# A six-layer cross network on one core: two row blocks stored singly, seventeen row loads, and narrower remainder evictions

## The chip, the core and the metric

The kernel runs on one core of a Trainium2 chip. A core has several engines that run their own instruction streams side by side: TensorE (PE) multiplies matrices into PSUM, VectorE (DVE) does elementwise work, ScalarE (ACT) does elementwise work and here mostly copies PSUM into SBUF ("evicts" it), GpSimd (POOL) does a little setup, and SyncE (SP) issues DMA transfers. Sixteen DMA engines carry the transfers. The metric is the device time of one execution in microseconds (us), taken as the median of several runs.

## The reference

The input x0 has 4096 rows and 416 columns (26 fields of 16). There are six weight matrices of 416 x 416 and six bias rows. All is bf16.

```python
def reference(x0, ws, bs):
    x = x0
    for l in range(ws.shape[0]):
        x = x0 * (x @ ws[l] + bs[l]) + x
    return x
```

Each layer multiplies the state x with a weight matrix, adds a bias, multiplies elementwise with x0 and adds the state of before.

## The kernel before, in words

The kernel doesn't carry x from layer to layer but a factor c with x = x0 * c: c starts from 1 and each layer adds the product and the bias to it. So a layer is three steps: TensorE forms x @ ws[l] in PSUM; ScalarE evicts it with the bias added (tile `t`); VectorE adds it to c and multiplies c by x0 to get the next x.

In layers 0 to 4 the data is transposed: columns of x lie on the 128 partitions, batch rows along the free dimension. The 416 columns are three full groups of 128 (index `m`, tiles `XM0`, `XH`, `CM`) and a remainder of 32 (tiles `XR`, `CR`). The 4096 batch rows are two halves (index `s`), each of four runs of 512 (index `g`). The remainder of 32 columns is packed: the four runs of one half lie on four blocks of 32 partitions, so that the remainder of a half is one tile of 128 x 512.

Layer 0 is `first_layer`, layers 1 to 3 are the loop with `layer_products`, `ew_main` (the full groups) and `ew_rem` (the remainder), and layer 4 is `feeding_layer`, which also sends the finished c through DMA transposes into row order (`XLrows`).

In layers 1 to 3 the order is: two products (one for each of the first two tiles) with their evictions, then `rem_pair`, which forms the remainder products of both halves in one PSUM tile of two banks and then runs `ew_rem` for each half, and then the other four tiles. `ew_rem` (lines 190 to 204) evicts the 512 columns of a half in pieces of `n` columns (line 197), and then VectorE adds all 512 columns to `CR` (line 203) and multiplies them (line 204). Before the change the pieces are 256 columns, and 128 for half 1 in layers 1 and 2. PSUM is used as four tiles of two banks, in turn, so the tile of the remainder products is taken again by the second tile of products after it; TensorE's first write into it there is a row product (line 215).

Layer 5 (`l = LL`) is formed in row order, 128 batch rows to a PSUM bank: 32 row blocks in four rounds of eight banks. For each row block the steps are a product on TensorE (lines 464 to 481), a copy out of PSUM by ScalarE (line 519, in the first round line 496), an addition of the row-ordered c (`XLrows`, line 523), a multiplication with the x0 rows (`X0rows`, line 505), and a store (line 508). The x0 rows come through a loop of loads at line 133, issued on SP behind the loads of the weights.

Several things set the order of the work. VectorE's instructions in the last layer and a few others are pinned to program order (`pin`). The rest is ordered by the framework's scheduler, by dependence and planned time, when the program is built. The multiplication and store of a row block are put off by one step: `close_product` runs when the next row block has been evicted and added. Stores are issued on SP, the very last one on ScalarE's queue. Transfers take eight completion semaphores in turn, and a transfer first waits for the one that had its semaphore before.

In the last round (`final`, `q` of 6) the row blocks are closed one by one. A tile `o` holds two of them, and before the change blocks 0 and 1, 2 and 3, 4 and 5 share a tile and a store; blocks 6 and 7 have their own. The lines that decide this are:

```python
paired = final and u < 6
j = u % 2 if paired else 0
if not j:
    outs.append(opool.tile([P, 2, D], BF16, name="o"))
```

`j` is the place in the tile, and the store is issued with the second of a pair or with a single block. Blocks 5, 6 and 7 get their c added on TensorE (lines 468 and 470), so VectorE only multiplies there, and block 7 is multiplied straight out of PSUM.

Of the kernel before, what the change touches and what calls it, by code (L numbers as in the profile page):

```python
# [16 lines left out]
def kernel(  # L17
# [16 lines left out]
    CW = 512  # L34
    SW = NG * CW
    NBT = B // P
# [36 lines left out]
    def load_wm(eng, l):  # L73
        eng.dma_start(WM[:, l], ws[l, 0:NK * P, :].rearrange("(k p) n -> p k n", p=P))
# [5 lines left out]
    def pin(ins):  # L80
        tc.keep_in_program_order(ins)
# [46 lines left out]
        load_wr(nc.sync, g, 1, L)  # L128
    for l in range(2, L):
        load_wm(nc.sync, l)  # L130
    for q in range(18):
        b0, b1 = NBT * q // 18, NBT * (q + 1) // 18
        nc.sync.dma_start(X0rows[:, b0:b1, :], x0_v[:, b0:b1, :])
    for g in range(NG):
        nc.sync.dma_start(bLr[32 * g:32 * g + 1, :], bs[LL:LL + 1, :])
# [55 lines left out]
    def ew_rem(l, s, pr, nxtR):  # L191
        cols = slice(CW * s, CW * s + CW)
        halves = [slice(a, a + CW // 2) for a in range(0, CW, CW // 2)]
        base = CR[:, cols] if l == 0 else tpool.tile([P, 2 * CW], BF16, name="t")
        n = CW // (4 if s and l in (1, 2) else 2)
        for a in range(0, CW, n):
            nc.scalar.activation(base[:, a:a + n], pr[:, a:a + n], ACT.Identity, bias=bR[:, l:l + 1], scale=1.0)  # L197
        if l == 0:
            for a in halves:
                part = slice(CW * s + a.start, CW * s + a.stop)  # L200
                pin(nc.vector.tensor_tensor(out=nxtR[:, part], in0=CR[:, part], in1=XR[0][:, part], op=ALU.mult))
            return
        nc.vector.tensor_tensor(out=CR[:, cols], in0=base[:, 0:CW], in1=CR[:, cols], op=ALU.add)
        nc.vector.tensor_tensor(out=nxtR[:, cols], in0=CR[:, cols], in1=XR[0][:, cols], op=ALU.mult)
# [30 lines left out]
    def first_layer(s):  # L235
# [53 lines left out]
        for m in range(2):  # L289
            ew_main(0, s, m, 1, pb[m], nxt)  # L290
        ew_rem(0, 0, pr[:, 0, :], nxtR)
        ew_main(0, s, 2, 1, pb[2], nxt)
        ew_rem(0, 1, pr[:, 1, :], nxtR)

    bias_setup()
# [4 lines left out]
    def rem_pair(l, cur, curR, nxtR):  # L300
        pr2 = psum.tile([P, 2, CW], FP32, tag="ps", name="pr2")
        for s in range(NS):
            mm_rem(l, s, pr2[:, s, :], cur, curR)
        for s in range(NS):
            ew_rem(l, s, pr2[:, s, :], nxtR)
# [140 lines left out]
    l = LL  # L446
# [8 lines left out]
    def mm_q_open(q, g, py):  # L455
        for k in range(NK):
            for j in range(0, P, 32):
                nc.tensor.matmul(py[j:j + 32, 0:D], lhsT=q_x(q, g, k)[:, j:j + 32], rhs=WM[:, l, k, :],  # L458
                                 start=(k == 0), stop=False, tile_position=(0, j))

    def mm_q_full(q, g, py, closes, adds=False):
        s, i = quads[q]
        for k in range(NK):
            nc.tensor.matmul(py[:, 0:D], lhsT=q_x(q, g, k), rhs=WM[:, l, k, :],  # L464
                             start=((not closes) and k == 0), stop=(closes and not adds and k == NK - 1))
            if adds:
                c0 = col0(s, g) + 128 * i
                nc.tensor.matmul(py[:, P * k:P * k + P], lhsT=CM[:, k, c0:c0 + 128], rhs=ident[:], start=False, stop=False)
        if adds:
            nc.tensor.matmul(py[:, NK * P:D], lhsT=CR[:, CW * s + 128 * i:CW * s + 128 * i + 128],  # L470
                             rhs=ident[:, 32 * g:32 * g + 32], start=False, stop=True)

    def mm_q_rem(q, py, done):
        s, i = quads[q]
        biased = q == NQ - 1
        for g in range(NG):
            nc.tensor.matmul(py[g][:, 0:D], lhsT=curR[32 * g:32 * g + 32, CW * s + 128 * i:CW * s + 128 * i + 128],  # L477
                             rhs=WR[32 * g:32 * g + 32, l, :], start=(g >= done), stop=(not biased and g < done),
                             tile_position=(32 * g, 0))
        for g in range(NG if biased else 0):  # L480
            nc.tensor.matmul(py[g][:, 0:D], lhsT=ones[32 * g:32 * g + 1, :],
                             rhs=bLr[32 * g:32 * g + 1, :], start=False, stop=(g < done), tile_position=(32 * g, 0))
# [10 lines left out]
    def evict_quad(u, src):  # L493
        q, g0 = u // 4, u % 4
        w = wide[:, q, 0:NG * D].rearrange("p (g d) -> p g d", g=NG)
        nc.scalar.copy(w[:, g0:g0 + 2, :], src)
        if g0 + 2 == NG:
            close_product()
            pin(nc.vector.tensor_tensor(out=w, in0=w, in1=XLrows[:, rows(q, 0, NG), :], op=ALU.add))
            pending.append((w, q, 0, NG, w, 0, True, nc.sync))  # L500
# [9 lines left out]
    def ew(q, g0, srcs, o, j, last, eng, added, direct):  # L510
        if direct:
            close_product()
            pending.append((srcs[0], q, g0, 1, o, j, last, eng))
            return
        t = tpool.tile([P, 2 * CW], BF16, name="t")
        n = 0
        for src in srcs:
            w = src.shape[1]
            nc.scalar.copy(t[:, n * D:n * D + w * D].rearrange("p (a d) -> p a d", a=w), src)  # L519
            n += w  # L520
        tv = t[:, 0:n * D].rearrange("p (a d) -> p a d", a=n)
        if not added:
            pin(nc.vector.tensor_tensor(out=tv, in0=tv, in1=XLrows[:, rows(q, g0, n), :], op=ALU.add))  # L523
        close_product()
        pending.append((tv, q, g0, n, o, j, last, eng))
# [5 lines left out]
    for q, at, done in rounds:  # L531
        tiles = [psum.tile([P, 2, CW], FP32, tag="ps", name=f"py{n}") for n in range(4)]
        bank = [tiles[n][:, a, :] for n, a in at]

        final = q + 2 == NQ

        def close(groups):
            u = groups[0][0]
            srcs = [tiles[at[g[0]][0]][:, at[g[0]][1]:at[g[0]][1] + len(g), 0:D] for g in groups]
            if q == 0:  # L540
                evict_quad(u, srcs[0])
                return
            paired = final and u < 6
            j = u % 2 if paired else 0
            if not j:
                outs.append(opool.tile([P, 2, D], BF16, name="o"))
            ew(q + u // 4, u % 4, srcs, outs[-1], j, bool(j) or not paired, nc.scalar if final and u == 7 else nc.sync,
               final and u >= 5, final and u == 7)

        for u in range(done):  # L550
            if q == 0:
                mm_q_open(q, u, bank[u])
            else:
                mm_q_full(q, u, bank[u], False)
        mm_q_rem(q, bank[0:4], done)
        close([range(done)])
        mm_q_rem(q + 1, bank[4:8], 0)
        for u in range(done, 8):
            mm_q_full(q + u // 4, u % 4, bank[u], True, final and u >= 5)
            if at is ENDS:  # L560
                close([[u]])
            elif u % 2:
                close([[u - 1, u]] if at is PAIRS else [[u - 1], [u]])
                if q == 0 and u == 3:
                    last_rows_out()
# [31 lines left out]
```

## Time and profile before

| what | value |
|---|---|
| median of the runs shown | 128.73 us (128.63 to 128.79, 3 runs) |
| the profiled execution | 129.13 us |
| its span in the trace | 127.3 us |
| TensorE busy | 122.9 us, 97% of the span |
| VectorE busy | 102.3 us, 80% |
| ScalarE busy | 88.2 us, 69% |
| DMA | 16.37 MB, 129 GB/s over the span |
| mean granted TensorE clock | 0.995 of full speed |

The span runs from the first to the last instruction in the trace; the execution's own time is longer by what lies around it. "Busy" is time in which an engine runs an instruction; being busy doesn't mean that the engine decides the time. The chain is followed backward from the last instruction, at each step to what released it. Lines such as L197 are line numbers of the kernel. A line of the time order reads: start, duration, engine, line, operation, output and input tiles, how many were merged, and in brackets the idle time ahead of it with what ended it. "SPq" and "ACTq" are those engines' instructions that issue transfers.

### The profile page before, as it was taken

How to read it: one execution, taken by the hardware profiler on the slowest of the kernel's cores; microseconds unless marked ns; L12 is line 12 of the kernel's file. 1: busy time of each engine (PE TensorE's matmuls, PEld its weight loads, DVE VectorE, ACT ScalarE, POOL GpSimd, SP SyncE). 2: the span in 40 equal slices, each digit the busy share in tenths (PEclk: the TensorE clock that was granted, in tenths of full speed). 3: DMA queues.
4: the chain of work that ended last, by engine and by line, in shares of the span. 5: the costliest groups of instructions: out<-in, count | busy, mean ns of one | idle time of the engine just before them, and what ended most of it. 6: DMA issues, size and time to landing. Idle time of an engine off the chain costs nothing.

```text
span 127.3 us, 3935 instructions
## 1 busy us (share of the span) xinstructions
PE 122.9 (97%) x1682; PEld 55.2 (43%) x1682; DVE 102.3 (80%) x188; ACT 88.2 (69%) x113; POOL 5.2 (4%) x18
## 2 busy tenths in 40 slices
PE   7999999999999999999999999999999999999980
PEld 3243343354435444534453444344435445445450
DVE  0023679774989898998898998898999999999990
ACT  0047866896869486869485859495859698679760
POOL 4004000500000000000000000000000000000000
PEclk9999999999999999999999999999999999999998
DMA  3999999999880000000000000000049999999865
GB/s 82 238 233 225 186 236 250 306 332 323 253 262 17 5 0 0 8 0 5 0 5 0 5 0 0 5 0 5 0 80 140 197 104 231 171 248 322 268 224 178
DMA packets 42229, 16.37 MB, mean 129 GB/s; under 512 B 31034, under 2 KB 42212, under 8 KB 42212
## 3 DMA queue, kind: packets, MB, share of 16 engines
q1 hardware_dynamic: 37432, 15.40, 53.2%
q10 hardware_dynamic: 4780, 0.72, 3.7%
q8 instruction: 13, 0.21, 0.8%
q14 instruction: 4, 0.03, 0.1%
HBM read 6.15 MB, written 3.41 MB: 75 GB/s over the span
## 4 chain that ended last, share of the span: by engine, by line
PE 88%; DVE 5%; DMA 2%; ACT 1%; DVEq 1%; issue 1%
PE pt L209 50%; PE ph L241 13%; PE py L464 6%; PE pt L215 5%; PE pr L225 5%; PE wps L148 4%; DVE o L505 2%; DVE t L523 2%; DMA out_dram<-XH 2%; PE pr L221 2%; PE ph L248 2%; PE py L458 1%; PE py L477 1%; ACT t L519 1%; DVEq L592 1%
## 5 line engine op out<-in xcount | busy, mean ns | idle before, releaser
L209 PE MATMUL pt<-XH,WM 128*32 128x512 bf16 x1152 | 65.2, 379 | 0.0
L187 ACT ACTIVATE t<-pt,bM 128x1024 bf16<-128x1024 f32 x36 | 37.1, 1114 | 13.1 <-PE pt L215 13.1
L209 PEld LDWEIGHTS <-WM 128*32 128x32 bf16 x1152 | 29.7, 97 | 33.8 <-issue 5.1
L188 DVE TENSOR_TENSOR CM<-t,CM 128x1024 bf16<-128x1024 bf16 x36 | 24.7, 687 | 4.3 <-ACT t L187 4.3
L189 DVE TENSOR_TENSOR XH<-CM,XM 128x1024 bf16<-128x1024 bf16 x36 | 24.9, 692 | 2.6
L464 PE MATMUL py<-WM,XH 128*128 128x416 bf16 x90 | 17.0, 339 | 0.0
L241 PE MATMUL ph<-XM,WM 128*128 128x512 bf16 x72 | 16.5, 381 | 0.0
L333 ACT ACTIVATE t<-pt,bM 128x1024 bf16<-128x1024 f32 x12 | 12.4, 1114 | 4.1 <-PE pt L215 4.1
L181 ACT ACTIVATE CM<-ph,bM 128x1024 bf16<-128x1024 f32 x12 | 12.5, 1112 | 3.5 <-PE ph L248 3.5
L519 ACT CAST t<-py 128x416 bf16<-128x416 f32 (+1 forms) x18 | 10.8, 601 | 3.3 <-PE py L464 1.4
L183 DVE TENSOR_TENSOR XH<-CM,XM 128x512 bf16<-128x512 bf16 x24 | 8.8, 429 | 4.1 <-ACT CM L181 4.1
L464 PEld LDWEIGHTS <-XH 128*128 128x128 bf16 x90 | 8.5, 98 | 7.5 <-issue 1.2
L241 PEld LDWEIGHTS <-WM 128*128 128x128 bf16 x72 | 6.7, 98 | 8.5 <-issue 1.3
L341 DVE TENSOR_TENSOR CM<-t,CM 128x1024 bf16<-128x1024 bf16 x12 | 8.0, 688 | 0.3 <-ACT t L333 0.3
L345 DVE TENSOR_TENSOR XH<-CM,XM 128x2048 bf16<-128x2048 bf16 (+1 forms) x7 | 7.5, 1069 | 0.2
L215 PE MATMUL pt<-XR,WR 32*128 32x512 bf16 x96 | 7.3, 379 | 0.0
L505 DVE TENSOR_TENSOR o<-t,X0rows 128x832 bf16<-128x832 bf16 (+1 forms) x15 | 7.1, 485 | 0.0
L225 PE MATMUL pr<-XH,WM 128*32 128x512 bf16 x96 | 6.6, 379 | 0.0
L523 DVE TENSOR_TENSOR t<-t,XLrows 128x832 bf16<-128x832 bf16 (+1 forms) x13 | 6.5, 502 | 0.0
L197 ACT ACTIVATE t<-pr,bR 128x256 bf16<-128x256 f32 (+1 forms) x16 | 5.3, 426 | 1.6 <-PE pr L225 1.6
L114 ACT ACT_TABLE_LOAD x1 | 1.3, 1283 | 6.2 <-DMA XM<-in_x_dram 6.2
L157 DVE CAST bM<-pb 128x18 f32<-128x18 bf16 x1 | 0.2, 177 | 5.6 <-PE pb L156 5.6
(64 smaller groups left out, 69.7 us busy)
## 6 DMA issues: line engine op xcount, KB each, us to landing
X0rows<-in_x_dram SPq DMA_DIRECT2D x14, 208.0 KB, 4.0
out_dram<-o SPq DMA_DIRECT2D x11, 208.0 KB, 3.7
WM<-in_ws_dram SPq DMA_DIRECT2D x5, 312.0 KB, 6.2
out_dram<-XH SPq DMA_DIRECT2D x4, 208.0 KB, 2.6
WR<-in_ws_dram SPq DMA_DIRECT2D x4, 130.0 KB, 4.0
X0rows<-in_x_dram SPq DMA_DIRECT2D x4, 104.0 KB, 5.8
WM<-in_ws_dram ACTq DMA_DIRECT2D x1, 312.0 KB, 3.4
XM<-in_x_dram SPq DMA_TRANSPOSE x8, 5.1
```

Source lines behind the costliest of these rows:

```text
L181: nc.scalar.activation(c, src, ACT.Identity, bias=bias, scale=1.0)
L187: nc.scalar.activation(t[:], src, ACT.Identity, bias=bias, scale=1.0)
L188: nc.vector.tensor_tensor(out=c, in0=t[:], in1=c, op=ALU.add)
L189: nc.vector.tensor_tensor(out=x, in0=c, in1=XM0[:, m, c0:c0 + 2 * CW], op=ALU.mult)
L209: nc.tensor.matmul(pts[g // 2][32 * q:32 * q + 32, g % 2, :], lhsT=WM[:, l, k, 128 * m + 32 * q:128 * m + 32 * q + 32], rhs=cur[s][:, k, C ...
L215: nc.tensor.matmul(pts[g // 2][:, g % 2, :], lhsT=WR[32 * g:32 * g + 32, l, 128 * m:128 * m + 128], rhs=curR[32 * g:32 * g + 32, CW * s:CW ...
L225: nc.tensor.matmul(pr[32 * g:32 * g + 32, :], lhsT=WM[:, l, k, NK * P:D], rhs=cur[s][:, k, CW * g:CW * g + CW], start=False, stop=(k == NK ...
L241: nc.tensor.matmul(pt[:, gl, :], lhsT=WM[:, 0, k, 128 * m:128 * m + 128], rhs=cur[:, k, c0:c0 + CW], start=(k == 0 and not after_row), sto ...
L333: nc.scalar.activation(ts[t + (h,)][:], pts[t][h][:].rearrange("p a b -> p (a b)"), ACT.Identity, bias=bM[:, t[1], l:l + 1], scale=1.0)
L464: nc.tensor.matmul(py[:, 0:D], lhsT=q_x(q, g, k), rhs=WM[:, l, k, :], start=((not closes) and k == 0), stop=(closes and not adds and k == ...
L505: pin(nc.vector.tensor_tensor(out=o[:, j:j + n, :], in0=src, in1=X0rows[:, rows(q, g0, n), :], op=ALU.mult))
L519: nc.scalar.copy(t[:, n * D:n * D + w * D].rearrange("p (a d) -> p a d", a=w), src)
```

## The change

The diff has three edits. The x0 rows are loaded by seventeen transfers instead of eighteen: fifteen of two row blocks and two of one, where there were fourteen of two and four of one. In `ew_rem` the pieces are now 128 columns also for half 0 of layer 2 and for both halves of layer 3, so these three evictions of 512 columns take four instructions instead of two; layer 1 stays as it was. In the last round the third and the fourth row block (u = 2 and 3) have a tile and a store of their own; the pairs 0 and 1, 4 and 5 stay.

```diff
@@ -128,8 +128,8 @@
-    for q in range(18):
-        b0, b1 = NBT * q // 18, NBT * (q + 1) // 18
+    for q in range(17):
+        b0, b1 = NBT * q // 17, NBT * (q + 1) // 17
         nc.sync.dma_start(X0rows[:, b0:b1, :], x0_v[:, b0:b1, :])
@@ -192,7 +192,7 @@
-        n = CW // (4 if s and l in (1, 2) else 2)
+        n = CW // (4 if l and (s or l > 1) else 2)
         for a in range(0, CW, n):
             nc.scalar.activation(base[:, a:a + n], pr[:, a:a + n], ACT.Identity, bias=bR[:, l:l + 1], scale=1.0)
@@ -540,7 +540,7 @@
-            paired = final and u < 6
+            paired = final and u in (0, 1, 4, 5)
             j = u % 2 if paired else 0
```

## The prediction

> **What bounds the kernel now.** I read the page first (busy shares, slices, chain), then the chain in order of time, then the two places that the diff touches: ScalarE and VectorE around the remainder evictions, and everything after 121 us. From the page:
>
> ```profile
> PE 122.9 (97%) x1682; PEld 55.2 (43%) x1682; DVE 102.3 (80%) x188; ACT 88.2 (69%) x113; POOL 5.2 (4%) x18
> DMA  3999999999880000000000000000049999999865
> PE 88%; DVE 5%; DMA 2%; ACT 1%; DVEq 1%; issue 1%
> ```
>
> TensorE is busy 97% and holds 88% of the chain. The DMA engines are full in two stretches only: the loads up to about 38 us and the stores and transposes from about 95 us. The chain in order of time, in layer 3 (the first layer is layer 0):
>
> ```profile
> 71.85 0.22 PE pr L221 x4
> 72.07 0.65 PE pr L225 x12
> 72.72 2.59 PE pt L209 x48
> 75.31 0.54 PE pt L215 x8
> 75.85 5.29 PE pt L209 x96
> ```
>
> Each piece starts where the last one ends: TensorE waits for nobody here. So nothing that ScalarE does in the middle layers shortens the time; it can only lengthen it, by making TensorE or VectorE wait. ScalarE by itself, in time order, in layers 2 and 3:
>
> ```profile
> 53.53 1.87 ACT L197 ACTIVATE t<-pr,bR 128x256 bf16<-128x256 f32 x6 [0.54 <-PE pr L225]
> 56.43 2.12 ACT L187 ACTIVATE t<-pt,bM 128x1024 bf16<-128x1024 f32 x2 [1.03 <-PE pt L215]
> ...
> 72.77 1.56 ACT L197 ACTIVATE t<-pr,bR 128x256 bf16<-128x256 f32 x4 [0.54 <-PE pr L225]
> 75.67 1.11 ACT L187 ACTIVATE t<-pt,bM 128x1024 bf16<-128x1024 f32 x1 [1.33 <-PE pt L215]
> ```
>
> The remainder evictions are followed by ScalarE idling 1.03 us and 1.33 us. VectorE takes their results here (layer 3):
>
> ```profile
> 74.78 0.42 DVE L203 TENSOR_TENSOR CR<-t,CR 128x512 bf16<-128x512 bf16 x1
> 75.24 0.42 DVE L204 TENSOR_TENSOR XR<-CR,XR 128x512 bf16<-128x512 bf16 x1
> 75.58 0.42 DVE L203 TENSOR_TENSOR CR<-t,CR 128x512 bf16<-128x512 bf16 x1
> ```
>
> The end, engines in time order, and the same stretch cut into windows (last two columns: busy share of the DMA engines, GB/s):
>
> ```profile
> 123.53 0.90 SPq L508 DMA_DIRECT2D out_dram<-o  x2
> 123.81 0.58 DVE L505 TENSOR_TENSOR o<-py,X0rows 128x416 bf16<-128x416 f32 x1
> 124.42 0.38 ACTq L508 DMA_DIRECT2D out_dram<-o  x1
> ```
>
> ```profile
> 122.80:123.40 0.60, 0.60 (x8) 0.39 (x7) 0.60 (x3) 0.43 (x2) 0.00 (x0) 1.00 0.94 311
> 123.40:123.80 0.40, 0.26 (x4) 0.10 (x1) 0.39 (x2) 0.08 (x1) 0.00 (x0) 1.00 0.12 35
> 123.80:124.40 0.60, 0.00 (x0) 0.00 (x0) 0.59 (x2) 0.00 (x0) 0.00 (x0) 1.00 0.93 297
> 124.40:125.90 1.50, 0.00 (x0) 0.00 (x0) 0.00 (x0) 0.00 (x0) 0.00 (x0) 1.00 0.96 309
> ```
>
> TensorE ends at 123.66, the last product at 124.39, the last store is issued at 124.42 and lands at 126.42; 0.84 us of closing work follow to 127.26. Between 123.80 and 125.90 the DMA engines are full, and just before, from 123.40 to 123.80, they stand at 0.12: the end is a short backlog of stores with a hole ahead of it.
>
> **The change, part by part.** (1) *Four evictions of 128 columns for two of 256, in three places:* batch half 0 of layer 2, both halves of layer 3. From the starts of the instructions in the trace, an eviction of 256 columns holds ScalarE for 0.36 us to the next start, one of 128 for 0.25 (their own durations: 0.47 and 0.38). A place costs 4 x 0.25 - 2 x 0.36 = 0.28 us of ScalarE. Layer 2: the last remainder eviction ends at 55.40 now, then at 55.68. Layer 3: 74.34 now; then 72.77 + 7 x 0.25 + 0.39 = 74.91. Who waits: ScalarE's next eviction starts at 56.43 and 75.67 (0.75 us still free in both); VectorE's second L203 at 75.58 (0.67 free; in layer 2 56.34, 0.66 free); TensorE's L215, which writes the buffer that these evictions release, at 56.07 and 75.31 at the earliest (0.39 and 0.40 free). All three covers stand, so I take 0. If all cover were gone it would cost 0.28 + 0.57 = 0.85 us, the upper end; no gain is possible, because TensorE has no gap to give back.
>
> (2) *Seventeen x0-row loads for eighteen.* SP issues the loads from 23.02 to 35.63 us and four small ones to 36.92, then waits 57.9 us for the first transpose of results. The bytes are the same, one issue (0.35 to 1.9 us of SP) goes. The first reader of these rows is VectorE's L505 at 109.43. Nothing is on the path: 0 from both sides. The count has one other use: transfers take their completion semaphores in turn, eight of them, and each transfer waits for the one eight before it. One load fewer and one store more leave the last store on the same semaphore as now, so the closing waits, which SP makes one after the other, keep their order.
>
> (3) *Third and fourth row block stored singly.* VectorE's instructions stay the same; one store more is issued on SP. Blocks 3 and 4 now leave together at 122.95, when the fourth product (122.56 + 0.37) is done. The third product starts at 121.99, so its block can leave at 121.99 + 0.37 + 0.03 = 122.39. SP issued the pair before at 121.81 for 0.37 us, so it is free at 122.19. A single store holds SP 0.44 us (the one at 123.99), until 122.83; the fourth block goes at 122.95 as now, and 123.53 and 123.99 behind it are not moved. Queued behind the new wait on SP are only those stores.
>
> What does it do to the landing? Data starts 0.91 us after issue (121.81 to 122.72, 122.95 to 123.87, by the packets). Block 3 would start at 123.30, follow the pair before it at 123.40, and fill 0.32 us of the hole. Then block 4 runs 123.87 to 124.19, the pair issued at 123.53 starts at 124.44 and needs 0.63, the next single 0.32, and the last store, whose first packet came at 125.44, ends 0.32 later at 125.76 instead of 125.91. So by the mean of the engines the gain is 0.15 us.
>
> But the mean hides one engine. A store is landed when sixteen engines have each reported, and in the trace one of the sixteen is late from 116.65 us on, where a 16 KB instruction fetch falls: it reports the store issued at 118.88 at 122.60, when the other fifteen were done at 121.17. From there it reports every 0.63 to 0.67 us a pair (122.60, 123.23, 123.87, 124.54, 125.17, 125.81) and then the singles after 0.32 and 0.29 (126.13, 126.42). It is never idle, so the hole isn't there for it; an earlier issue finds it still busy with earlier stores, and its bytes don't change. Its last report ends the kernel. By it the gain is only what two singles (0.32 + 0.29 = 0.61) take less than a pair (0.63): 0.02 us. Ends for this term: 0.32 us of gain (the hole used, 0.15 as above, and the late engine's surplus gone, its last report now 0.12 behind the others, with 0.05 us of spread in the reports) and 0.26 us of loss (below). I take 0.02, since the late engine is the one that ends the kernel.
>
> The sum: 0 + 0 - 0.02. The profiled execution took 129.13 us, 1.83 us over its span; it would take 129.11. The median of the runs shown is 0.40 lower, 128.73, and carries the same difference: **128.71**.
>
> A rule that speaks against the split: the Trainium skill, "DMA: Bandwidth & Descriptors", section "Rules for kernel authors", wants many small transfers coalesced, and its section "Anatomy of one DMA" gives a transfer (on another issuing path) a fixed cost of about 2.0 us whatever its size. Paid one after the other, that would make the sum about +2 us; the trace agrees with it as a latency (2.0 us from the last issue to its landing) and not as a time that a store keeps its engines.
>
> **The rivals.**
> - *The hole is filled for good.* If the late engine isn't late in most executions, the mean decides: 0.15 us less, 128.58. For it: the share of 0.12 between 123.40 and 123.80. Against: sixteen reports in a row without a pause.
> - *Hole and late engine both go:* 0.32 us, 128.41. For it: the sixteenth report is already only 0.12 behind at the end, having been 1.4 behind. Against: its bytes are fixed.
> - *The extra issue blocks SP* (the other side). Issues onto full DMA engines took up to 1.14 us (116.87). At that price the third block holds SP from 122.39 to 123.53, block 4 goes at 123.58 instead of 122.95, the pair at 123.99 instead of 123.53, the next at 124.41. Block 4's data starts at 124.49, the pair at 124.90 for 0.63, the single and the last store need 0.64 more: 126.17 against 125.91, 0.26 us later, 128.99. It decides from an issue of about 0.85 us on, where the pair behind it starts as late as its data can go out today. Against it: at 122.4 the engines are not full (0.55 of their time from 122.2 to 123.0).
> - *The remainder evictions lose their cover,* because the scheduler, given more pieces, puts VectorE's or TensorE's work in another order: up to 0.85 us, 129.58. Against it: layer 2 (256 and 128 columns) and layer 3 (256 alone) show the same order on VectorE, to 0.01 us.
> - *Each store keeps the queue for a fixed time beside its bytes:* with the 2.0 us from issue to landing as that time, 130.7. Against it: the two singles at the end follow each other by 0.29 us, less than half a pair's 0.63.
>
> **How the numbers follow.** Bound for a change: 0.2% is 0.26 us. The forecast 0.56 (own range 128.62 to 128.80, the spread of the runs shown around it); hole filled 0.15, of which 0.03 passes 0.2%; both gone 0.09; blocked SP 0.08, of which 0.05 passes 0.2%; cover lost 0.09; fixed time 0.03. So faster 0.12, slower 0.17, same 0.71. The range 128.40 to 129.00 reaches to both gone and to blocked SP; it leaves out the lost cover and the fixed time, 0.12, and a little at the ends.
>
> **What would show it.** Right: ScalarE's L197 evictions x8 from 53.53 and 72.77 ending near 55.7 and 74.9, with TensorE's pieces still end to end; seventeen loads; SP issues near 121.8, 122.4, 122.95, 123.5 and 124.0; the DMA share between 123.40 and 123.80 up to about 0.8, and the last landing still near 126.4. Wrong: an idle time of TensorE at L215, SP's issue at 122.4 lasting near a microsecond, VectorE's L203 and L188 in another order, or a last landing below 126.2 with the time lower by as much.

## The result and the profile after

The changed kernel takes 129.02 us (median of 21 runs, 128.75 to 129.49), the kernel before in the same comparison 128.73: ratio 1.0021, 95% interval 1.0013 to 1.0029. The forecast was 128.71, with a range up to 129.00. Two later comparisons of the same kernel came out at 1.0007 and 1.0004; the section on the experiments says what is settled and what isn't.

The profiled execution took 129.09 us (span 127.3). Its page, the lines that answer to those shown of before:

```profile
PE 122.2 (96%) x1682; PEld 55.2 (43%) x1682; DVE 102.3 (80%) x188; ACT 89.1 (70%) x119; POOL 5.2 (4%) x18
DMA  3999999999960000000000000000059999999884
PE 62%; DVE 21%; DMA 9%; issue 3%; SPq 1%; ACT 1%; DVEq 1%
```

ScalarE has six instructions and 0.9 us more, TensorE and VectorE the same counts. (The chain now names VectorE and DMA for part of the way. That is no sign of a new bound: in the two further profiles of the changed kernel told of below, TensorE has 90% and 68% of it, VectorE under 1% and 22%.) The middle layers, layer 3 in the chain in order of time:

```profile
72.05 0.65 PE pr L225 x12
72.69 2.59 PE pt L209 x48
75.28 0.54 PE pt L215 x8
75.83 4.20 PE pt L209 x73
```

and ScalarE and VectorE there, in time order:

```profile
53.51 2.17 ACT L197 ACTIVATE t<-pr,bR 128x128 bf16<-128x128 f32 x8 [0.54 <-PE pr L225]
56.41 2.12 ACT L187 ACTIVATE t<-pt,bM 128x1024 bf16<-128x1024 f32 x2 [0.73 <-PE pt L215]
...
72.75 2.17 ACT L197 ACTIVATE t<-pr,bR 128x128 bf16<-128x128 f32 x8 [0.53 <-PE pr L225]
75.65 2.12 ACT L187 ACTIVATE t<-pt,bM 128x1024 bf16<-128x1024 f32 x2 [0.73 <-PE pt L215]
```

```profile
74.76 0.42 DVE L203 TENSOR_TENSOR CR<-t,CR 128x512 bf16<-128x512 bf16 x1
75.21 0.42 DVE L204 TENSOR_TENSOR XR<-CR,XR 128x512 bf16<-128x512 bf16 x1
75.55 0.42 DVE L203 TENSOR_TENSOR CR<-t,CR 128x512 bf16<-128x512 bf16 x1
```

All as forecast: the evictions end at 55.68 and 74.92, 0.73 us of cover are left, TensorE's pieces stand end to end, and VectorE's L203 starts where it did. From the first product of layer 1 (line 209) to TensorE's last instruction it is 97.15 us in both kernels. The loss isn't there. The end, engines in time order, and its windows (last two columns: DMA share, GB/s):

```profile
123.49 1.12 SPq L508 DMA_DIRECT2D out_dram<-o  x2
123.78 0.58 DVE L505 TENSOR_TENSOR o<-py,X0rows 128x416 bf16<-128x416 f32 x1
124.39 0.38 ACTq L508 DMA_DIRECT2D out_dram<-o  x1
```

```profile
122.80:123.40 0.60, 0.60 (x9) 0.36 (x6) 0.60 (x3) 0.45 (x1) 0.00 (x0) 1.00 1.06 326
123.40:123.80 0.40, 0.23 (x3) 0.10 (x1) 0.38 (x3) 0.06 (x1) 0.00 (x0) 1.00 0.78 250
123.80:124.40 0.60, 0.00 (x0) 0.00 (x0) 0.56 (x2) 0.00 (x0) 0.00 (x0) 1.00 0.56 182
124.40:125.90 1.50, 0.00 (x0) 0.00 (x0) 0.00 (x0) 0.00 (x0) 0.00 (x0) 1.00 0.81 265
```

The third row block did fill the hole from 123.40 to 123.80: 0.12 has become 0.78. But a new hole follows it (0.56 from 123.80 to 124.40, where it was 0.93), and SP's last two issues take 1.12 us instead of 0.90. By single instructions, the issue of the pair at 123.49 took 0.61 us where it took 0.37 before, so the next one went at 124.19 instead of 123.99. What stands beside it shows in the page's part on queues (packets, MB, share of the sixteen engines), before:

```profile
q14 instruction: 4, 0.03, 0.1%
```

and after:

```profile
q14 instruction: 5, 0.04, 0.1%
```

One more 8 KB instruction fetch. By the trace's packets it begins at 123.34 us and takes 0.64. In the kernel before the fetch in its place comes at 128.24, after the last instruction. The changed kernel has begun 192 ScalarE instructions when the fetch comes (its semaphore waits and transfer issues counted); the kernel before has only 191 in all.

The Trainium skill, "DMA: Bandwidth & Descriptors", section "Queues, rings and completion order", keeps one queue row, 14, for the runtime's own traffic and names refills among it. The trace agrees as far as ScalarE's fetches go (q14, kind "instruction"); TensorE's are on q8 here. What such a fetch costs a kernel's transfers is what the experiments are about.

### The profile page after: what moved, and what is told of

It is laid out like the page before. It is cut to its first block, busy times and chain, and to the rows that moved or that the text cites. A ratio compares the mean times of both kernels' runs of the same rounds, so it can differ in the third digit from the quotient of the medians.

```text
span 127.3 us, 3942 instructions
## 1 busy us (share of the span) xinstructions
PE 122.2 (96%) x1682; PEld 55.2 (43%) x1682; DVE 102.3 (80%) x188; ACT 89.1 (70%) x119; POOL 5.2 (4%) x18
## 4 chain that ended last, share of the span: by engine, by line
PE 62%; DVE 21%; DMA 9%; issue 3%; SPq 1%; ACT 1%; DVEq 1%
PE pt L209 39%; PE ph L241 11%; DVE XH L345 6%; DVE CM L341 5%; DMA XM<-in_x_dram 5%; PE pt L215 4%; PE pr L225 4%; DMA XLrows<-CM 3%; DVE o L505 3%; DVE t L523 3%; DVE CM L349 2%; PE ph L248 1%; PE pr L221 1%; SPq L78 1%; ACT t L333 1%
## 5 line engine op out<-in xcount | busy, mean ns | idle before, releaser
L209 PEld LDWEIGHTS <-WM 128*32 128x32 bf16 x1152 | 29.7, 97 | 33.8 <-issue 5.1
L197 ACT ACTIVATE t<-pr,bR 128x128 bf16<-128x128 f32 (+1 forms) x22 | 6.2, 389 | 1.6 <-PE pr L225 1.6
L225 PEld LDWEIGHTS <-WM 128*32 128x32 bf16 x120 | 3.2, 97 | 3.2
```

The source lines that it names most:

```text
L209: nc.tensor.matmul(pts[g // 2][32 * q:32 * q + 32, g % 2, :], lhsT=WM[:, l, k, 128 * m + 32 * q:128 * m + 32 * q + 32], rhs=cur[s][:, k, C ...
L225: nc.tensor.matmul(pr[32 * g:32 * g + 32, :], lhsT=WM[:, l, k, NK * P:D], rhs=cur[s][:, k, CW * g:CW * g + CW], start=False, stop=(k == NK ...
```

## The experiments

**Theory A:** the six extra ScalarE instructions bring the fetch into the last stores, and this is the loss. **Theory B:** the extra store lengthens the backlog. **Theory C,** formed after the first four runs: the count of the loads. **Theory D,** formed after the first eight: the narrow evictions themselves, fetch or no fetch. Each kernel was timed in five rounds beside the kernel before. All the trace readings are collected in one table behind the runs.

**Evictions alone.** Edit against the kernel before:

```diff
-        n = CW // (4 if s and l in (1, 2) else 2)
+        n = CW // (4 if l and (s or l > 1) else 2)
```

> The kernel before with the narrower remainder evictions alone: six instructions more on ScalarE (197 traced instead of 191), no other change. Theory A (instruction fetch): in the changed kernel an 8 KB instruction fetch stands at 123.34 us, when ScalarE has started 192 instructions, in the middle of the last stores; in the kernel before it comes after the end (128.24). By A this kernel has the fetch near 123.3 too and takes the whole loss: ratio about 1.002, 129.0 us. Theory B (the extra store lengthens the backlog at the end): no extra store here, ratio 1.000, 128.73 us. Either way the middle layers stay end to end on TensorE.

Measured: 128.83 us, ratio 1.0003 (0.9988 to 1.0019). The fetch stands at 123.11, the issue behind it takes 0.57 us, as A has it; the time leaves A's 1.002 just outside its interval and doesn't exclude 1.001.

**Stores alone.** Edit against the kernel before:

```diff
-            paired = final and u < 6
+            paired = final and u in (0, 1, 4, 5)
```

> The kernel before with the third and fourth row block of the last round stored singly, eighteen loads and the old evictions: 191 instructions on ScalarE. Theory A: no fetch before the end, ratio 0.999 to 1.000 (128.58 to 128.73 us), SP's issue near 123.5 us takes 0.37 us as before. Theory B: the whole loss is here, ratio about 1.002, and the issue near 123.5 us takes about 0.6 us as in the changed kernel.

Measured: 128.86 us, ratio 1.0006 (0.9996 to 1.0016). SP's issue takes 0.38 us, and no fetch comes before the end. The last landing is the earliest so far after the last issue, 1.85 us, but from there to the end it takes 0.94 us where the others take 0.83 to 0.84: without the load taken out, the last store has another semaphore of the turn, and the closing waits come in another order. So the price of B is this 0.10 us, seen in one profile, and one load fewer avoids it. B as a longer backlog falls.

**The change with six ScalarE instructions taken out elsewhere.** Edit against the changed kernel (line 197's pieces, line 369's and line 312's):

```diff
-        n = CW // (4 if l and (s or l > 1) else 2)
+        n = CW // ((2 if s else 1) if l == 1 else 4 if l else 2)
...
-        n = 4 if s else 2
+        n = 4
...
-            for a in range(0, CW, CW // 2):
+            for a in range(0, CW, CW):
```

> The changed kernel with six ScalarE instructions taken out elsewhere: remainder evictions of layer 4 in one piece instead of two (two fewer), of layer 1 in one and two pieces instead of two and four (three fewer), and the copy of the first half's row-ordered remainder in one instead of two (one fewer): 191 in all, extra store and seventeen loads kept. Theory A: the fetch is gone from the last stores and the loss with it, ratio 0.999 to 1.000 against the kernel before. Theory B: still 1.002.

Measured: 129.12 us, ratio 1.0019 (1.0000 to 1.0037), times from 128.59 to 129.92. No fetch, issue 0.38 us; and yet the last landing came 2.18 us after the last issue, because one of the sixteen DMA engines reported 0.31 us behind the other fifteen. A miss for A as a theory of the whole loss.

**The kernel before again.**

> The kernel before, unchanged, for a second profile and the spread of its times: ratio 1.000 within 0.05%. Its first profiled execution took 129.13 us, 0.4 us over its median. Under theory A and B alike, no fetch stands between 122 and 126 us; if the profiled execution now is near 128.7 us, the place where the two executions differ tells what varies from run to run.

Measured: 128.81 us, ratio 0.9996 (0.9985 to 1.0006). Its profiled execution took 128.78 us, 0.35 less than the one that the prediction was read from. They differ at two places: TensorE reaches layer 1 at 26.29 instead of 26.51, and the late DMA engine, which ended the first execution by reporting 0.12 us behind the others, is here only 0.02 behind.

**Loads alone,** and **loads and stores.** Edit against the kernel before, without and with the edit to the stores:

```diff
-    for q in range(18):
-        b0, b1 = NBT * q // 18, NBT * (q + 1) // 18
+    for q in range(17):
+        b0, b1 = NBT * q // 17, NBT * (q + 1) // 17
```

> The kernel before with seventeen x0-row loads alone (191 ScalarE instructions, old stores). Theory A (the fetch near 123.3 us is the loss): none here, ratio 1.000. Theory C (the count of the loads is the loss, since the two kernels so far with seventeen loads stand at 1.002 and 1.002 and those with eighteen at 1.000 to 1.001): ratio about 1.002. One load fewer and no store more puts the last store on another semaphore of the turn: if that costs what it cost with the extra store alone (0.94 us from the last landing to the end against 0.83 to 0.84), the ratio is 1.0008 under A.

> Seventeen loads and the single stores, old evictions (191 ScalarE instructions): the changed kernel without the fetch in the last stores. Theory A: ratio 0.999 to 1.000, 0.83 us from the last landing to the end, SP's issue near 123.5 us 0.37 us long. Theory C: 1.002, the same as the changed kernel.

Measured: loads alone 128.82 us, 1.0001 (0.9992 to 1.0010), closing 0.89 us; loads and stores 128.71 us, 0.9996 (0.9984 to 1.0007), closing 0.84. Theory C falls. It was formed from two kernels that happened to share the seventeen loads; they share the narrower evictions too.

**The changed kernel again.**

> The changed kernel again, beside the others on one chip: ratio 1.002 as before (1.0013 to 1.0029). If it comes out at 1.000, what was measured belongs to that loading of the program and not to the change. The profile should again show the fetch near 123.3 us and the issue behind it near 0.6 us long.

Measured: 128.91 us, ratio 1.0007 (0.9998 to 1.0016). The interval leaves out the first 1.0021 and holds 1.000, so by the expectation's own test a part of what was measured first belongs to that loading of the program. Here the fetch came at 123.29, only 0.01 us ahead of SP's issue, and didn't hold it (0.38 us); the last landing was still late (1.98 us).

**Eight more ScalarE instructions,** to move the fetch. Edit against the changed kernel:

```diff
-        n = CW // (4 if l and (s or l > 1) else 2)
+        n = CW // (4 if not l or s or l > 1 else 2)
...
-            for a in range(0, CW, CW // 2):
+            for a in range(0, CW, CW // 4):
```

> The changed kernel with eight more ScalarE instructions: the remainder evictions of layers 0 and 4 in pieces of 128 columns too, 205 instead of 197. ScalarE reaches its 192nd instruction some 2.5 us earlier, so by theory A the fetch moves to about 120.8 us and no longer stands ahead of the last four stores: ratio back to 1.000 to 1.001. Theory C: 1.002, wherever the fetch stands.

Measured: 128.92 us, ratio 1.0010 (1.0000 to 1.0021). The fetch near 123.3 is gone, and no issue was held. There are two fetches now, at 121.16 and 121.39, with 194 and 196 ScalarE instructions begun; one of them is ScalarE's, and the trace doesn't tell which, because every other profile has one between 121.10 and 121.95 as well. The last landing came 1.99 us after the last issue, 0.14 later than without a fetch, but the trace shows another reason for that: the edit took the cover away in layer 4, where ScalarE's evictions (line 369) now take 2.17 us instead of 1.57. VectorE's first addition there (line 374) starts 66.68 us after the first product of layer 1, where all the other profiles have 66.47, and VectorE makes up only a part of it: the last pair of row blocks is stored at 97.14 us by that clock instead of 97.00 to 97.02. From that pair's issue to the last report it takes 2.79 us, hardly more than the 2.75 to 2.78 of eight profiles without the fetch. So the time, neither theory's number, has a third cause in it, the lost cover of the prediction's rival, at another place.

**Six evictions of one column,** the kernel before otherwise unchanged, and the same with the loads and stores. Edit:

```diff
-        for a in range(0, CW, n):
-            nc.scalar.activation(base[:, a:a + n], pr[:, a:a + n], ...)
+        for a, to, w in [(a, base[:, a:a + n], n) for a in range(0, CW, n)] + [(0, dy[:], 1)] * (1 if l else 0):
+            nc.scalar.activation(to, pr[:, a:a + w], ...)
```

> The kernel before, all three edits undone, with six evictions of one column added on ScalarE (one in each remainder eviction of layers 1 to 3, into a tile that nobody reads): 197 instructions on ScalarE, as many as in the changed kernel. Theory A (the 192nd instruction brings an 8 KB fetch into the last stores): a fetch near 123.2 us, the last landing 0.1 to 0.25 us later after the last issue than the 1.85 us of the kernels without it, 0.09 us less outside the span; ratio 1.0005 to 1.0015. Theory D (narrow evictions themselves do it, fetch or no fetch): ratio 1.000 and a last landing 1.85 us after the last issue.

> Seventeen loads, single stores, and the six evictions of one column in place of the narrower evictions. Theory A: the same time as the changed kernel, 0.1 to 0.2 us over the kernel with the loads and stores alone in the same comparison. Theory D: no difference to that one.

Measured: 128.81 us, 0.9997 (0.9984 to 1.0010), and 128.71 us, 0.9997 (0.9983 to 1.0011). In both profiles the fetch is there at the 192nd instruction (123.07 and 123.50), the issue behind it takes 0.55 and 0.72 us, and the last landing is 1.99 and 2.15 us after the last issue: the mechanism of A without any further narrow eviction. The times don't follow: no loss.

**Loads and stores again, and the change with six instructions taken out at other places.** The second edit, against the changed kernel (beside line 369 and line 312 as above):

```diff
-        n = CW // (4 if l and (s or l > 1) else 2)
+        n = CW // (1 if not l or (l == 1 and not s) else 4)
```

> Seventeen loads and single stores again, without the narrower evictions: ratio 0.9990 to 1.0005 (0.9996 the first time), a last landing 1.85 us after the last issue, no fetch between 122 us and the end.

> The changed kernel with six ScalarE instructions taken out at other places than the first time: remainder evictions of layers 0 and 4 in one piece of 512 columns (four fewer), the first half's in layer 1 in one (one fewer), one copy for two in the row-ordered remainder (one fewer); 191 instructions with the narrower evictions kept. Theory A: no fetch in the last stores, ratio 0.999 to 1.0005, last landing 1.85 us after the last issue. Theory D: ratio 1.001 to 1.002 and a late landing as in the first such kernel (2.18 us).

Measured: 128.81 us, 0.9999 (0.9990 to 1.0007), and 128.74 us, 1.0001 (0.9988 to 1.0014). The second one keeps every narrow eviction of layers 2 and 3, has 191 ScalarE instructions, no fetch, and its last landing 1.85 us after the last issue. So D falls for the landing: narrow evictions without the fetch don't delay it.

**The crossing, once more in one comparison.**

> The changed kernel a third time. Theory A, with what the profiles show by now: a fetch inside the last stores puts the last landing 0.1 to 0.3 us later and takes 0.09 us off the time outside the span, net 0 to 0.2 us, ratio 1.000 to 1.0015. If the first comparison (1.0021) is the change's own, the ratio is 1.0013 or more again.

> Seventeen loads and single stores without the narrower evictions, a third time: ratio 0.9990 to 1.0005; by theory A below the changed kernel in this comparison by 0.05 to 0.2 us.

> The same with the six evictions of one column: by theory A (the fetch) as slow as the changed kernel in this comparison; by theory D (the narrower evictions themselves) as fast as the loads and stores alone.

> The narrower evictions kept and 191 instructions: by theory A as fast as the loads and stores alone, by theory D as slow as the changed kernel.

Measured: the changed kernel 128.85 us, 1.0004 (0.9993 to 1.0015); loads and stores 128.70, 1.0000 (0.9990 to 1.0011); with six tiny evictions 128.65, 0.9994 (0.9983 to 1.0006); narrow evictions without the fetch 128.90, 1.0008 (0.9995 to 1.0020). In the times A isn't seen: a kernel with the fetch is the fastest. The two kernels with the narrower evictions stand above the two without, the order that D asks for, but the intervals overlap. In the profiles the fetch and the late landing go together in all four.

The traces together, us. "To layer 1" is the start of the first product of layer 1; from there to TensorE's last instruction it is 97.15 to 97.16 in all eighteen, and 0.76 (0.78 once) more to the last store's issue. "Landing" is from that issue to the last report; "closing" from there to the last instruction; "outside" is the execution's own time less that. A row's time is the sum of 97.15, 0.76 and the four terms.

| kernel | ScalarE instructions | fetch at | SP issue behind it | to layer 1 | landing | closing | outside | its time |
|---|---|---|---|---|---|---|---|---|
| before, first | 191 | 128.24 | 0.37 | 26.51 | 2.00 | 0.84 | 1.87 | 129.13 |
| before again | 191 | 128.12 | 0.37 | 26.29 | 1.87 | 0.83 | 1.87 | 128.78 |
| loads | 191 | 128.41 | 0.37 | 26.55 | 1.86 | 0.89 | 1.87 | 129.09 |
| stores | 191 | 127.97 | 0.38 | 26.29 | 1.85 | 0.94 | 1.90 | 128.89 |
| loads, stores | 191 | 127.83 | 0.38 | 26.25 | 1.85 | 0.84 | 1.90 | 128.76 |
| loads, stores, again | 191 | 127.78 | 0.38 | 26.17 | 1.85 | 0.84 | 1.89 | 128.66 |
| loads, stores, third | 191 | 128.53 | 0.38 | 26.94 | 1.85 | 0.83 | 1.89 | 129.43 |
| change less six, first way | 191 | 128.32 | 0.38 | 26.42 | 2.18 | 0.84 | 1.87 | 129.22 |
| change less six, other way | 191 | 127.90 | 0.38 | 26.30 | 1.85 | 0.83 | 1.87 | 128.77 |
| the same, again | 191 | 128.00 | 0.38 | 26.42 | 1.86 | 0.84 | 1.87 | 128.90 |
| changed | 197 | 123.34 | 0.61 | 26.48 | 2.07 | 0.84 | 1.78 | 129.09 |
| changed, again | 197 | 123.29 | 0.38 | 26.30 | 1.98 | 0.83 | 1.81 | 128.83 |
| changed, third | 197 | 123.63 | 0.38 | 26.32 | 2.21 | 0.83 | 1.79 | 129.06 |
| evictions | 197 | 123.11 | 0.57 | 26.26 | 2.10 | 0.83 | 1.81 | 128.92 |
| six tiny | 197 | 123.07 | 0.55 | 26.20 | 1.99 | 0.84 | 1.78 | 128.73 |
| loads, stores, six tiny | 197 | 123.50 | 0.72 | 26.59 | 2.15 | 0.83 | 1.78 | 129.27 |
| the same, again | 197 | 123.06 | 0.60 | 26.22 | 2.02 | 0.83 | 1.78 | 128.76 |
| change plus eight | 205 | 121.39 | 0.38 | 26.17 | 1.99 | 0.84 | 1.78 | 128.70 |

Five things can be read from these runs.

*The fetch follows the count.* In all seven profiles with 197 ScalarE instructions the trace shows 192 of them begun when the fetch comes; with 191 the fetch comes after the end; with 205 it comes 2 us earlier, at 194 or 196 begun (the table has the later of the two fetches there). An earlier one on the same queue comes at 62 to 65 begun ScalarE instructions in every profile, some 128 fewer.

*It holds SP's issue.* In the five profiles where the fetch began 0.10 to 0.18 us before SP's issue, that issue ended 0.13 to 0.15 us after the fetch did (changed: fetch to 123.98, issue to 124.10; evictions: 123.69 and 123.84; six tiny: 123.61 and 123.76; with loads and stores: 124.20 and 124.33, then 123.71 and 123.84). These five fetches took 0.54 to 0.70 us. Where the fetch began 0.01 us before the issue, or after it, the issue took 0.38; and in the changed kernel's third profile, where the next issue began 0.18 us behind a fetch of only 0.31 us, it took its usual 0.42. SP's issues that run between 122.0 and 124.9 us, by line (ns: least, median, greatest; then first and last start). With the fetch (loads, stores, six tiny, second profile):

```profile
L508 SPq DMA_DIRECT2D out_dram<-o x4: 344/381/597, 122.1 to 123.9; - x4
```

and without (change less six, other way, second profile):

```profile
L508 SPq DMA_DIRECT2D out_dram<-o x5: 344/372/417, 121.7 to 123.9; - x5
```

*What it is worth.* The last landing takes 1.85 to 1.87 us after the last issue in eight of ten profiles without the fetch and 1.98 to 2.21 in the seven with it at 197 instructions: later by 0.11 to 0.36. Where the issue was held, all sixteen DMA engines report late: the first report comes 1.80 to 1.96 us after the last issue, against 1.66 to 1.69 in the ten without the fetch. In the changed kernel's second and third profile the first report is on time (1.68 and 1.66) and only the last engines are late. Two of the ten without the fetch show that too (2.00 and 2.18), so there it may be chance. About 0.09 us come back: with 191 instructions the time outside the span is 1.87 to 1.90, with the fetch inside the run it is 1.78 to 1.81. Changed kernel (means of three) against loads and stores (means of three): landing 2.09 against 1.85, closing 0.83 and 0.84, outside 1.79 against 1.89, so 0.13 us slower by the profiles. Against the kernel before, second profile: 0.14.

*The spread is at the start.* "To layer 1" runs from 26.17 to 26.94, with the same program too (loads and stores: 26.17, 26.25, 26.94). The chain in order of time of the slow one:

```profile
2.97 5.91 DMA xrig<-in_x_dram
8.88 0.05 issue
8.93 0.23 PE tpr L163
9.15 0.04 issue
9.20 0.23 PE tpr L163
9.43 2.08 PE ph L241 x9
```

and of the kernel before, second profile:

```profile
6.40 2.13 PE ph L241 x9
8.53 0.11 PE tpr L161
8.64 0.33 PE tpr L163 x4
8.97 1.94 PE ph L241 x9
```

In the first, TensorE waits for the load of the x0 remainder, which took 5.9 us; in the second it was there. No edit touches this, and it is larger than anything that the edits do.

*The times follow the narrower evictions, not the fetch.* The eight comparisons of kernels with narrower evictions in layers 2 and 3 lie at 1.0001 to 1.0021, the nine of kernels without them at 0.9994 to 1.0006. Means, weighted by the runs:

| | with the fetch | without it |
|---|---|---|
| narrower evictions | 1.0011 (5 comparisons) | 1.0009 (3) |
| the wider ones of before | 0.9996 (3) | 1.0000 (6) |

So over all runs theory D fits the times, by about 0.1%, though not the landing, and theory A fits the landing, though not the times. This grouping was made when all results were in, no kernel was run to test it, and the 1.0010 of the eight more instructions has the lost cover in it. Nor do the profiles say where such a loss would lie: two of the three kernels with narrow evictions and no fetch land at 1.85 and 1.86 us like the others.

What is settled and what isn't: that the count of ScalarE instructions brings the fetch into the last stores, and that the fetch holds an issue and delays the landing, is shown. That this is the measured loss is not shown. The three comparisons of the changed kernel, weighted by their runs (21, 12, 11), give (21 x 1.0021 + 12 x 1.0007 + 11 x 1.0004) / 44 = 1.0013, 0.17 us; the profiles' 0.13 us are of that size. But the kernels with six tiny evictions, with the same late landing, are not slower in their times (three comparisons, 0.9994 to 0.9997); eight of their 36 times lie at 128.36 to 128.52, where the least of the kernel before in these comparisons is 128.59, and no profile caught such an execution. The changed kernels with the fetch taken out stand at 1.0001 and 1.0008 in one form and 1.0019 in the other, which doesn't show the loss gone. Open too is why the first comparison showed more than the two later ones. No version beats the kernel before clearly: loads and stores without the evictions stand at 0.9996, 0.9999 and 1.0000.

## Why the prediction was wrong

The forecast, 128.71 us, was 0.31 below the measured time and on the other side of no change.

- **The evictions (part 1): this step failed.** Its local mechanism was right: the evictions end at 55.68 and 74.92, all covers stand, TensorE has no gap. What failed is the conclusion "All three covers stand, so I take 0", a term put at nothing from the place where the instructions run alone. The kernels with the narrower evictions average 1.0010, 0.13 us, and those without them 0.9998. One effect away from that place is shown: six more instructions put the 192nd ScalarE instruction, and the 8 KB fetch that comes with it, into the last stores, where the profiles show the landing 0.11 to 0.36 us later and 0.09 us back outside the span. But kernels with the same fetch and no narrower evictions lost no time, so what makes up the measured loss stays open, and so does the larger part of the first comparison's 0.29 us.
- **The loads (part 2): right.** Loads alone stand at 1.0001. That the count keeps the last store on its semaphore was told; that this is worth 0.10 us (stores alone, closing 0.94 against 0.84) wasn't priced; it rests on one profile.
- **The single stores (part 3): right in size, by a wrong reason.** Forecast 0.02 us of gain; landing goes from 1.87 (before again) to 1.85. But the late DMA engine that I let decide was a mark of that one execution: in the second profile of before it had caught up and the landing was still 1.87. What limits the gain is the pair of row blocks behind, issued near 123.3 us as before, whose data can't be out much earlier. With loads and stores alone the hole only moves ahead of that pair, and from there to the end the DMA engines are full:

```profile
123.90:124.20 0.30, 0.00 (x0) 0.00 (x0) 0.23 (x1) 0.00 (x0) 0.00 (x0) 1.00 0.16 44
124.30:125.40 1.10, 0.00 (x0) 0.00 (x0) 0.00 (x0) 0.00 (x0) 0.00 (x0) 1.00 1.01 315
```

  Against before again, the pair's first report comes 0.07 us sooner after its issue (1.88 for 1.95), the next single's 0.03 (1.76 for 1.79), the last store's 0.01 (1.67 for 1.68).
- **The rivals.** "The hole is filled for good" (128.58) had the place right, the DMA share rose as it said, and the gain wrong, for the reason just given. "The extra issue blocks SP" named a wait that did appear, of 0.24 us, but in another issue (the pair at 123.49, not the third block at 122.35, which took 0.34) and for another cause. The lost cover didn't come in this kernel. Neither did the fixed time for each store, nor what the rule of coalescing would make of it (the Trainium skill, "DMA: Bandwidth & Descriptors", section "Rules for kernel authors"): the kernel with one store more lands no later. That rule's own mark of 64 KB lies under both sizes of store here, 104 and 208 KB, so it hardly bears on this split.
- **The basis.** The forecast was made from one execution of 129.13 us, 0.40 over the median. Half of that was its start (0.22 us) and a third its late DMA engine (0.13); I carried it over as a constant and read the engine as the rule. (The time outside the span, 1.83 us in the prediction, is 1.87 with the span's end at 127.26.)

## What to carry to other kernels

Instruction fetches stand among the DMA packets of the trace, and ScalarE's came at nearly the same count of its instructions in every profile that reached it (62 to 65, then 192 to 196): before adding a few, count how many have begun when the fetches come, and look which stretch the next one will fall into. At the end of a kernel, ask which issue the last stretch of full DMA engines starts from; what is sent ahead of it has nothing to give. One profile tells the shape of an end, not its size: a second one of the same program showed which of its features were chance. And an effect that a profile shows isn't yet the loss that the times show: put the two in one table, with every kernel that has the one without the other.

## What the hardware showed that I had not expected

- ScalarE's instructions come in fetches of 8 KB, seen at 62 to 65 and at 192 begun instructions (194 or 196 in the kernel with 205); TensorE's come in 16 KB on a queue of their own, q8, thirteen in each profile for some 3370 instructions.
- A store's issue on SP that began 0.10 to 0.18 us after the start of a fetch of 0.54 to 0.70 us wasn't done until 0.13 to 0.15 us after the fetch ended (five of five profiles); it takes 0.37 to 0.38 us alone. An issue that began later in a fetch, or behind a shorter one, was not longer than usual.
- The time outside the span is 0.06 to 0.12 us shorter (1.78 to 1.81 against 1.87 to 1.90) when the last fetch falls inside the run instead of after it.
- With one transfer more or less ahead of it, the last store lands on another semaphore of the turn, and the closing takes 0.89 or 0.94 us instead of 0.83 to 0.84 (one profile each).
